# W_O read in joined pieces, the last V in one load, and a selection in two parts: an attention decode kernel on Trainium2

## The chip, the cores and the metric

One core of one Trainium2 chip. Its engines run their own instruction streams beside each other and meet at semaphores: TensorE (PE; PEld is its weight load) multiplies, VectorE (DVE), ScalarE (ACT) and GpSimd (POOL) work on elements, SyncE (SP) issues loads to 16 DMA engines. The metric is the device time of one execution in microseconds (us), lower is better. Times of before: 195.54 us, median of 3 runs (195.34 to 196.03).

## The reference

One decode step for 4 sequences: grouped-query attention over the last 4096 cached positions, plus a SwiGLU feed-forward, both on the same normalized input, plus the input itself.

```python
def _A_ref(x, k_cache, v_cache, wq, wo):      
    W = min(4096, max(256, Sk // 4))
    q = (x @ wq).reshape(B, Sq, Hq, Dh).transpose(0, 2, 1, 3)
    k = jnp.repeat(k_cache[:, :, Sk - W:, :], rep, axis=1)
    v = jnp.repeat(v_cache[:, :, Sk - W:, :], rep, axis=1)
    p = _softmax(jnp.einsum("bhqd,bhkd->bhqk", q, k) * (Dh ** -0.5))
    o = jnp.einsum("bhqk,bhkd->bhqd", p, v)
    return o.transpose(0, 2, 1, 3).reshape(B, Sq, Hq * Dh) @ wo
def _B_ref(x, w_gate, w_up, w_down):
    return (_silu(x @ w_gate) * (x @ w_up)) @ w_down
...
return x + _A_ref(xn, ...) + _B_ref(xn, ...)
```

Here W = 4096, Hq = 32, eight key heads, Dh = 128, D = 512 and F = 1792. The keys and values that are used are 2 x 32 MB, the weights some 13 MB, all bf16.

## The kernel before, in words

**The loads.** All large loads go through SyncE's one queue, in the order written in its function: W_Q, the first two K, W_gate, W_up, then V and K in turn, W_down, the last V, W_O. A K or a V load ("piece" d of ND = 16) is 2 MB: two sequences of one key head. K is double-buffered by TensorE's count of transposes (s_tr), V by the count of finished P times V (s_pv). The helper load (L174) issues a load whose destination is written by partition (16 KB each for K and V) and whose source is named in longer runs (32 KB: FOLD = 2 partitions' worth), by replacing the source's access pattern. K, V and the three feed-forward weights go through it. Two loads don't: the last V, which load_v_half (L250) issues as four loads of 512 KB, two for each half of the positions, with semaphores d_v[1] and d_vz, so that the first half can be used while the second is on its way; and W_O, which load_wo (L257) issues as five loads.

**W_O's layout.** wo_ap (L167) puts rows 32p to 32p + 31 of W_O into partition p, one after another: W_O's 4096 rows are 128 partitions times NO = 32 rows. What is called row c in this document is that c-th row of all partitions, a 128 x 512 operand. WO_CUTS (L123) cuts the 32 rows into loads: 0 to 15, 16 to 25, 26 to 28, 29 and 30, 31.

**The loop.** For each d, TensorE transposes K (L407), VectorE copies it back (L321), TensorE makes scores, a row maximum is taken, ScalarE takes the exponential (L292), and TensorE forms the denominators and P times V. The loop runs 8 times over two d; behind it stand gate and up products, the last denominators and P times V (L482 to L484, which wait for d_v[1] and d_vz), and the 28 products of the down projection.

**The end.** OT holds the attention output with the head's 128 dimensions across the partitions, one column per head and sequence. But row c of W_O in partition p belongs to row 32p + c of W_O, that is to head p // 4, dimension 32 (p % 4) + c. So the output must be regrouped: four transposes (L492) turn OT into tr_ps with 32 heads across the partitions, VectorE copies it to OB (L372), and four selecting products (L498), with the tables of ones and zeros in rep, spread it into op_ps, 128 partitions by 32 rows by 4 sequences; VectorE copies that to OP (L374). out_rows (L189) then multiplies OP's row c by W_O's row c, two products each, waiting for a W_O load at each cut. Rows 0 to 15 come inside the Block, the others behind it; at the Block's end the engines meet. spin (L445) issues filler products whose result nobody reads: two behind the transposes, three behind the selecting products, three behind row 15. At last y is copied by VectorE and ScalarE (L511, L513) and stored.

The table rep is made by GpSimd at the start (L206, L220), ahead of s_const, for which TensorE's first transposes wait.

Of the kernel before, what the change touches and what calls it, by code (L numbers as in the profile page):

```python
# [7 lines left out]
ALU = mybir.AluOpType  # L8
# [4 lines left out]
def bass_parallel_sum__sliding_block_cached__swiglu_ffn__decode_kernel(  # L13
# [32 lines left out]
    WIDE = 64  # L46
    PS = SN + WIDE
    NO = HQ * Dh // 128
    SCALE = float(Dh) ** -0.5
    EPS = 1e-5  # L50
# [16 lines left out]
    ones = sb("ones", [128, 128], BF16)  # L67
    rep = sb("rep", [32, REP, 128], BF16)
    mkr = sb("mkr", [2, 128], BF16)
# [16 lines left out]
    OT = sb("oT", [128, B, REP + HQ], BF16)  # L86
    OB = sb("oB", [32, B, Dh], BF16)
    OP = sb("oP", [128, NO, B], BF16)
    ex = sb("ex", [128, NF, B], FP32)
    guT = sb("guT", [128, NF, B], BF16)  # L90
    qT = KT[:, 0:2048].bitcast(FP32)
    gT = WQ[:, 0:NF * 64].bitcast(FP32)
    uT = WQ[:, NF * 64:NF * 128].bitcast(FP32)
    I4 = sb("i4", [B, B], FP32)
    I4w = sb("i4w", [B, 64], BF16)
# [15 lines left out]
    up_ps = ps_kt[1][:, 0:NF * 32]  # L111
    tr_ps = kt_ps[2][0:32, 0:B, :]
    op_ps = ps_kt[3][:, 0:B * 32]

    def sem(name):
        return nc.alloc_semaphore(name=name)
# [5 lines left out]
    d_out = sem("d_out")  # L122
    WO_CUTS = (0, 16, 26, 29, 31, 32)  # L123
    d_wo = [sem("d_wo%d" % q) for q in range(len(WO_CUTS) - 1)]
    d_k = [sem("d_k%d" % s) for s in range(2)]
    d_v = [sem("d_v%d" % s) for s in range(2)]
    d_vz = sem("d_vz")
    s_const = sem("s_const")
# [24 lines left out]
    s_guT = sem("s_guT")  # L153
    s_t4 = sem("s_t4")
    s_ob = sem("s_ob")
    s_pm = sem("s_pm")
# [9 lines left out]
    wd_ap = B_w_down.rearrange("(p t) n -> p t n", t=NF)  # L166
    wo_ap = A_wo.rearrange("(p c) n -> p c n", c=NO)  # L167
# [21 lines left out]
    def out_rows(eng, c0, c1):  # L189
        for c in range(c0, c1):  # L190
            if c in WO_CUTS:
                eng.wait_ge(d_wo[WO_CUTS.index(c)], 16)
            for n in range(2):
                last = eng.matmul(ps_acc[64 * n:64 * n + B, 0:256], OP[:, c, :], WO[:, c, 256 * n:256 * n + 256],  # L194
                                  start=False, stop=True, skip_group_check=True)
        return last

    with nc.Block() as block:

        @block.gpsimd  # L200
        def _(eng):
# [3 lines left out]
            eng.memset(I4w[:], 0.0)  # L205
            eng.memset(rep[:], 0.0)  # L206
            eng.memset(ones[:], 1.0)
# [10 lines left out]
                              fill=1.0, base=0, channel_multiplier=1)  # L218

            eng.affine_select(rep[:], rep[:], pattern=[[1, REP], [-1, 128]], compare_op=ALU.not_equal,  # L220
                              fill=1.0, base=0, channel_multiplier=REP)

# [14 lines left out]
            eng.engine_nop().then_inc(d_v[1], 16)  # L237

        @block.sync
        def _(eng):  # L240
# [8 lines left out]

            def load_v_half(d, h, done):  # L250

                a = d % 2 * KVN + h * HKN
                for i in range(FOLD):
                    b = i * KVN + h * HKN
                    eng.dma_start(VB[i:128:FOLD, a:a + HKN], kv_ap(A_v_cache, d, FOLD)[:, :, b:b + HKN]).then_inc(done, 16)

            def load_wo(n):  # L257
                a, b = WO_CUTS[n], WO_CUTS[n + 1]
                eng.dma_start(WO[:, a:b, :], wo_ap[:, a:b, :]).then_inc(d_wo[n], 16)

# [11 lines left out]
            load(eng, WD[:], wd_ap, fold_rows(B_w_down)).then_inc(d_wd, 16)  # L272
            eng.wait_ge(s_pv, ND)
            load_v_half(ND - 1, 0, d_v[1])
            load_v_half(ND - 1, 1, d_vz)
            for n in range(len(d_wo)):
# [20 lines left out]
        def _(eng):  # L297
# [74 lines left out]
            eng.tensor_copy(OB[:], tr_ps).then_inc(s_ob, 1)  # L372
            eng.wait_ge(s_pm, 1)
            eng.tensor_copy(OP[:].rearrange("p c b -> p b c"), op_ps.rearrange("p (b c) -> p b c", b=B)).then_inc(s_op, 1)  # L374

        @block.tensor
        def _(eng):
# [102 lines left out]
            for n in range(2):  # L480
                mm(ps_acc[64 * n:64 * n + 64, 0:256], I4w[:], X[:, 256 * n:256 * n + 256], start=True)
            pv(1, 0, (8 * ND + 16 * FOLD, ND + 1))  # L482
            eng.wait_ge(d_vz, 16 * FOLD)
            pv(1, 1, None)  # L484
# [18 lines left out]
            eng.wait_ge(s_op, 1)  # L503
            out_rows(eng, 0, WO_CUTS[1])
            spin(3)

# [38 lines left out]
```

## Time and profile before

| what | value |
|---|---|
| median of 3 runs | 195.54 us (195.34 to 196.03) |
| the profiled execution | 195.45 us, of which its span is 194.2 us |
| TensorE busy, of the span | 164.6 us, 85% |
| VectorE busy | 115.3 us, 59% |
| ScalarE, GpSimd busy | 17.0 us, 10.5 us |
| moved by DMA | 81.10 MB, mean 418 GB/s over the span |
| loads of K, of V (first 15) | 2048 KB each, landed 12.5 and 11.2 us behind their issue |

The span goes from the first to the last instruction that the profiler recorded. In the page's rows an engine is busy when an instruction of it runs; matmuls are pipelined, so that a busy TensorE is not one at its peak, and which engine bounds the kernel has to be read from what waits for what.

### The profile page before, as it was taken

The page shows a single profiled execution, that of the slowest core. Times are in us where ns is not written, and L with a number is a line of the kernel's source. Part 1 is how long each engine was busy: PE and PEld are TensorE (multiplying, and loading weights), DVE is VectorE, ACT ScalarE, POOL GpSimd, SP SyncE. Part 2 cuts the span into 40 slices and gives each one's busy share as a digit, 9 for nine tenths or more (in the row PEclk, how much of TensorE's full clock was granted, in tenths as well). Part 3 has the DMA queues.
Part 4 walks back from the last instruction along what each step waited for, and adds up shares of the span by engine and source line. Part 5 has one row for each costly group of instructions (what it writes and reads, how often), then busy time and mean ns, then how long its engine had stood idle before and what let it go on. Part 6 is the DMA issues. An engine that isn't in the chain of part 4 may idle for free. (4 is left out here: it accounts for less than half of the span.)

```text
span 194.2 us, 7760 instructions
## 1 busy us (share of the span) xinstructions
PE 164.6 (85%) x3466; PEld 141.6 (73%) x3466; DVE 115.3 (59%) x250; ACT 17.0 (9%) x27; POOL 10.5 (5%) x23
## 2 busy tenths in 40 slices
PE   0127999739999989898989898989898989898995
PEld 0112988638989888888888887888788878887752
DVE  1004858517677767676767676767676767675610
ACT  6600010100110101010101010101010101010100
POOL 8930000000000000000000000000000000000000
PEclk9999999988999999999999999999999999999999
DMA  6999998999999999999999999999999999998992
GB/s 224 425 439 432 564 393 346 425 430 439 412 432 432 432 432 432 432 432 432 432 432 432 432 432 439 432 452 432 432 432 432 432 439 432 432 472 353 437 407 107
DMA packets 3830, 81.10 MB, mean 418 GB/s; under 512 B 712, under 2 KB 848, under 8 KB 1104
## 3 DMA queue, kind: packets, MB, share of 16 engines
q1 hardware_dynamic: 3808, 81.01, 97.4%
q8 instruction: 5, 0.08, 0.2%
q10 hardware_dynamic: 16, 0.01, 0.0%
q14 instruction: 1, 0.01, 0.0%
HBM read 81.01 MB, written 0.00 MB: 417 GB/s over the span
## 5 line engine op out<-in xcount | busy, mean ns | idle before, releaser
L321 DVE COPY kT<-ps_kt 128x1024 bf16<-128x1024 bf16 x128 | 79.9, 683 | 28.0 <-PE ps_kt L407 28.0
L407 PE MATMUL ps_kt<-ident,kbuf 128*128 128x128 bf16 x1024 | 65.6, 224 | 11.2 <-DMA kbuf<-in_A_k_cache_dram 10.3
L407 PEld LDWEIGHTS ps_kt<-ident,kbuf 128*128 128x128 bf16 x1024 | 60.0, 101 | 16.5 <-issue 16.5
L379 PE MATMUL ps_o<-p,vbuf 128*128 128x64 bf16 x1120 | 38.4, 193 | 0.0
L379 PEld LDWEIGHTS ps_s<-qz,kT 128*128 128x128 bf16 x1024 | 31.4, 98 | 6.8 <-issue 3.6
L379 PEld LDWEIGHTS ps_o<-p,vbuf 128*128 128x128 bf16 x1120 | 35.2, 98 | 1.1
L379 PE MATMUL ps_s<-qz,kT 128*128 x1024 | 34.8, 192 | 1.2
L292 ACT ACTIVATE p<-ps_s 128x512 bf16<-128x512 f32 x17 | 10.2, 597 | 161.9 <-PE ps_s L379 161.9
L326 DVE TENSOR_REDUCE rm<-ps_s 128x8 bf16<-128x512 f32 x17 | 11.8, 691 | 19.9 <-PE ps_s L379 19.9
L379 PE MATMUL ps_kt<-wq_sb,xnT 128*32 128x512 bf16 x32 | 3.6, 629 | 5.5 <-DMA wq_sb<-in_A_wq_dram 5.5
L379 PE MATMUL ps_o<-p,ones 128*128 128x128 bf16 (+1 forms) x69 | 7.0, 222 | 1.6 <-DVE qz L312 1.3
L379 PE MATMUL ps_s<-mkc,mkr 2*128 2x512 bf16 x17 | 6.8, 398 | 0.0
L384 PE MATMUL ps_acc<-i,xn 4*128 4x4 f32 x4 | 0.6, 254 | 7.1 <-ACT xn L289 7.1
L379 PE MATMUL ps_s<-dg,ones 8*128 8x512 bf16 x17 | 6.5, 385 | 0.0
L379 PEld LDWEIGHTS ps_o<-p,ones 128*128 128x128 bf16 x69 | 4.5, 98 | 2.7 <-issue 2.2
L379 PEld LDWEIGHTS ps_kt<-wq_sb,xnT 128*32 128x32 bf16 x32 | 1.2, 137 | 7.1 <-issue 7.1
L309 DVE STREAM_TRANSPOSE kT<-ps_kt 128x512 f32<-128x512 f32 x2 | 1.4, 718 | 8.3 <-PE ps_kt L379 8.3
L384 PEld LDWEIGHTS ps_acc<-i,xn 4*128 4x128 f32 x4 | 0.6, 207 | 7.0 <-issue 7.0
L337 DVE TENSOR_REDUCE den<-ps_o 128x8 f32<-128x128 f32 x18 | 5.0, 275 | 1.0 <-PE ps_o L379 1.0
L234 POOL MEMSET vbuf<- 128x6144 f32 x1 | 5.2, 5222 | 0.0
L331 DVE TENSOR_REDUCE m<-ps_acc 8x1 f32<-8x128 f32 x17 | 4.6, 270 | 0.3 <-PE ps_acc L379 0.3
L341 DVE TENSOR_TENSOR oT<-ps_o,den 128x8 f32 (+1 forms) x18 | 3.0, 167 | 2.9 <-issue 2.7
(68 smaller groups left out, 50.5 us busy)
## 6 DMA issues: line engine op xcount, KB each, us to landing
kbuf<-in_A_k_cache_dram SPq DMA_DIRECT2D x16, 2048.0 KB, 12.5
vbuf<-in_A_v_cache_dram SPq DMA_DIRECT2D x15, 2048.0 KB, 11.2
wq_sb<-in_A_wq_dram SPq DMA_DIRECT2D x1, 4096.0 KB, 12.3
vbuf<-in_A_v_cache_dram SPq DMA_DIRECT2D x4, 512.0 KB, 7.8
wo_sb<-in_A_wo_dram SPq DMA_DIRECT2D x1, 2048.0 KB, 13.3
wg_sb<-in_B_w_gate_dram SPq DMA_DIRECT2D x1, 1792.0 KB, 24.1
wu_sb<-in_B_w_up_dram SPq DMA_DIRECT2D x1, 1792.0 KB, 27.5
wd_sb<-in_B_w_down_dram SPq DMA_DIRECT2D x1, 1792.0 KB, 14.9
```

What stands on the lines that cost most here:

```text
L234: eng.memset(VB[:, HKN:].bitcast(FP32), 0.0)
L292: eng.activation(P[:, d % 2 * PS:d % 2 * PS + SN], ps_S[d % 2][:], ACT.Exp, scale=SCALE).then_inc(s_p, 1)
L309: eng.transpose(qT[:, 512 * n:512 * n + 512], ps_kt[n][:])
L321: eng.tensor_copy(KT[:, u * HKN + 1024 * g:u * HKN + 1024 * (g + 1)], kt_ps[g].rearrange("p a b -> p (a b)")).then_inc(s_ev, 1)
L326: eng.tensor_reduce(RM[:], ps_S[bank][:].rearrange("p (t c) -> p c t", c=C), AX.X, ALU.max).then_inc(s_rm, 1)
L331: eng.tensor_reduce(m8[:], mt_ps, AX.X, ALU.max)
L337: eng.tensor_reduce(den[:], den_ps.rearrange("p (t c) -> p c t", c=C), AX.X, ALU.add)
L341: eng.tensor_tensor(OT[:, 2 * b:2 * b + 2, ds(r * REP, REP)], O_ps.rearrange("p (j h) -> p j h", j=2), den[:].rearrange("p (j h) -> p j h" ...
L379: return eng.matmul(o, l, r, start=start, stop=stop, skip_group_check=True)
L384: last = eng.transpose(xT_ps[:, c * B:(c + 1) * B], xn[:].rearrange("b (p c) -> b c p", c=NC)[:, c, :], I4[:])
L407: last = eng.transpose(kt_ps[g][:, k, :], KB[:, a:a + 128], ident[:])
```

## The change

- **Layout of W_O.** Rows 0 to 15 of a partition are now 16 neighbouring rows out of W_O's first 2048; rows 16 to 23 are 8 neighbouring rows out of the next 1024; rows 24 to 31 are one row of each of the last eight heads, 128 rows of W_O per load. The cuts become 0, 16, 24, 29, 31, 32; the last eight rows are eight loads that add to three semaphores.
- **Reads.** All W_O loads go through load: the first two name the source in runs of 32 KB, the last eight in 16 runs of 8 KB, with 1 KB written to each partition.
- **The last V** goes through load_v like the others: one load, one semaphore; d_vz is gone.
- **The regrouping.** The last eight heads need none: their operand is OT itself. The other NP = 24 are transposed, copied and selected in two parts (RUNS): 8 products with 64 columns for rows 0 to 15, then 16 products with 32 columns for rows 16 to 23, each part with its own copy to OP.
- **Fillers.** The three behind the selecting products and the three behind row 15 are gone; the two behind the transposes stay.
- **The tables** are made by GpSimd behind the Q projection (it waits for s_q = 2), in a part of WQ that is free by then; TensorE waits for s_rep ahead of the selecting.

```diff
+    RUNS = ((0, 16), (16, 8))
+    NP = 24
...
-    OB = sb("oB", [32, B, Dh], BF16)
-    OP = sb("oP", [128, NO, B], BF16)
+    OB = sb("oB", [NP, B, Dh], BF16)
+    OP = sb("oP", [128, NP, B], BF16)
...
+    rep_all = WQ[0:NP, NF * 128:NF * 128 + NP * 128]
+    rep = [rep_all[:, 1024 * n:1024 * n + 128 * (128 // r)].rearrange("a (e m) -> a e m", m=128)
+           for n, (_, r) in enumerate(RUNS)]
...
-    tr_ps = kt_ps[2][0:32, 0:B, :]
-    op_ps = ps_kt[3][:, 0:B * 32]
+    tr_ps = kt_ps[2][0:NP, 0:B, :]
+    op_ps = [t[:, 0:B * r].rearrange("p (b c) -> p b c", b=B) for t, (_, r) in zip((ps_kt[3], ps_kt[1]), RUNS)]
...
-    WO_CUTS = (0, 16, 26, 29, 31, 32)
+    WO_CUTS = (0, 16, 24, 29, 31, 32)
...
     def out_rows(eng, c0, c1):
         for c in range(c0, c1):
             if c in WO_CUTS:
-                eng.wait_ge(d_wo[WO_CUTS.index(c)], 16)
+                n = WO_CUTS.index(c)
+                eng.wait_ge(d_wo[n], 16 if c < NP else 16 * (WO_CUTS[n + 1] - c))
             for n in range(2):
-                last = eng.matmul(ps_acc[64 * n:64 * n + B, 0:256], OP[:, c, :], WO[:, c, 256 * n:256 * n + 256],
-                                  start=False, stop=True, skip_group_check=True)
+                last = eng.matmul(ps_acc[64 * n:64 * n + B, 0:256], OP[:, c, :] if c < NP else OT[:, :, REP + c],
+                                  WO[:, c, 256 * n:256 * n + 256], start=False, stop=True, skip_group_check=True)
...
         def _(eng):
-            eng.memset(rep[:], 0.0)
-            eng.affine_select(rep[:], rep[:], pattern=[[1, REP], [-1, 128]], compare_op=ALU.not_equal,
-                              fill=1.0, base=0, channel_multiplier=REP)
...
+            eng.wait_ge(s_q, 2)
+            eng.memset(rep_all.bitcast(FP32), 0.0)
+            eng.drain()
+            for (h, r), to in zip(RUNS, rep):
+                eng.affine_select(to, to, pattern=[[1, 128 // r], [-1, 128]], compare_op=ALU.not_equal,
+                                  fill=1.0, base=-128 // r * h, channel_multiplier=128 // r)
+            eng.drain()
+            eng.engine_nop().then_inc(s_rep, 1)
...
             def load_wo(n):
                 a, b = WO_CUTS[n], WO_CUTS[n + 1]
-                eng.dma_start(WO[:, a:b, :], wo_ap[:, a:b, :]).then_inc(d_wo[n], 16)
+                if a < NP:
+                    w = A_wo[128 * a:128 * b, :]
+                    load(eng, WO[:, a:b, :], w.rearrange("(p c) n -> p c n", p=128),
+                         w.rearrange("(p c) n -> p (c n)", c=32)).then_inc(d_wo[n], 16)
+                    return
+                for c in range(a, b):
+                    w = A_wo[128 * c:128 * c + 128, :]
+                    load(eng, WO[:, c, :], w, w.rearrange("(p c) n -> p (c n)", p=16)).then_inc(d_wo[n], 16)
...
-            eng.wait_ge(s_pv, ND)
-            load_v_half(ND - 1, 0, d_v[1])
-            load_v_half(ND - 1, 1, d_vz)
+            load_v(ND - 1)
...
-            eng.wait_ge(s_pm, 1)
-            eng.tensor_copy(OP[:].rearrange("p c b -> p b c"), op_ps.rearrange("p (b c) -> p b c", b=B)).then_inc(s_op, 1)
+            for n, (h, r) in enumerate(RUNS):
+                eng.wait_ge(s_pm, n + 1)
+                eng.tensor_copy(OP[:, h:h + r, :].rearrange("p c b -> p b c"), op_ps[n]).then_inc(s_op, 1)
...
-            pv(1, 0, (8 * ND + 16 * FOLD, ND + 1))
-            eng.wait_ge(d_vz, 16 * FOLD)
+            pv(1, 0, (8 * ND + 16, ND + 1))
             pv(1, 1, None)
...
-                    OT[:, i, REP:], ident[:])
+                    OT[:, i, REP:REP + NP], ident[:])
             last.then_inc(s_t4, 1)
             spin(2)
+            eng.wait_ge(s_rep, 1)
             eng.wait_ge(s_ob, 1)
-            for e in range(REP):
-                last = mm(op_ps.rearrange("p (b c) -> p b c", b=B), rep[:, e, :], OB[:, :, 32 * e:32 * e + 32],
-                          start=(e == 0))
-            last.then_inc(s_pm, 1)
-            spin(3)
+            for n, (h, r) in enumerate(RUNS):
+                for e in range(128 // r):
+                    last = mm(op_ps[n], rep[n][:, e, :], OB[:, :, r * e:r * e + r], start=(e == 0))
+                last.then_inc(s_pm, 1)
             eng.wait_ge(s_op, 1)
             out_rows(eng, 0, WO_CUTS[1])
-            spin(3)
+            eng.wait_ge(s_op, 2)
```

More of the change, by code (lines that the diff above doesn't have):

```diff
@@ L67, in bass_parallel_sum__sliding_block_cached__swiglu_ffn__decode_kernel @@
     ones = sb("ones", [128, 128], BF16)
-    rep = sb("rep", [32, REP, 128], BF16)
     mkr = sb("mkr", [2, 128], BF16)
@@ L126, in bass_parallel_sum__sliding_block_cached__swiglu_ffn__decode_kernel @@
     d_v = [sem("d_v%d" % s) for s in range(2)]
-    d_vz = sem("d_vz")
     s_const = sem("s_const")
@@ L154, in bass_parallel_sum__sliding_block_cached__swiglu_ffn__decode_kernel @@
     s_t4 = sem("s_t4")
+    s_rep = sem("s_rep")
     s_ob = sem("s_ob")
@@ L166, in bass_parallel_sum__sliding_block_cached__swiglu_ffn__decode_kernel @@
     wd_ap = B_w_down.rearrange("(p t) n -> p t n", t=NF)
-    wo_ap = A_wo.rearrange("(p c) n -> p c n", c=NO)
     ds = bass.ds
@@ L248, in load_v @@
                 load_kv(eng, VB, A_v_cache, d).then_inc(d_v[d % 2], 16)
[L250 to L255, printed above, removed]
             def load_wo(n):
                 a, b = WO_CUTS[n], WO_CUTS[n + 1]
-                eng.dma_start(WO[:, a:b, :], wo_ap[:, a:b, :]).then_inc(d_wo[n], 16)
+                if a < NP:
[6 more added lines that the diff above has]
+                    load(eng, WO[:, c, :], w, w.rearrange("(p c) n -> p (c n)", p=16)).then_inc(d_wo[n], 16)
             eng.dma_start(WQ[:], wq_ap).then_inc(d_wq, 16)
```

## The prediction

> **What bounds the kernel now.** I began with the head of the page and its DMA rows, to see which resource is never free.
>
> ```profile
> span 194.2 us, 7760 instructions
> GB/s 224 425 439 432 564 393 346 425 430 439 412 432 432 432 432 432 432 432 432 432 432 432 432 432 439 432 452 432 432 432 432 432 439 432 432 472 353 437 407 107
> q1 hardware_dynamic: 3808, 81.01, 97.4%
> q8 instruction: 5, 0.08, 0.2%
> PE ps_acc L194 1%; DVE y_sb L511 0%
> ```
>
> The loads issued by SyncE keep all 16 DMA engines busy for 97.4% of the span, at a flat 432 GB/s until the last slice. The page's chain is 1% long: it stops where the last W_O products begin, because what released them is a load. So I read the tail by itself, in the timeline (start, duration, engine, line, what; in brackets the idle time before and its releaser):
>
> ```profile
> 187.33 1.65 PEld L194 LDWEIGHTS ps_acc<-wo_sb,oP 128*4 128x4 bf16 x32 [0.65 <-DVE oP L374]
> 187.36 1.91 PE L194 MATMUL ps_acc<-wo_sb,oP 128*4 128x256 bf16 x32 [0.19 <-DMA wo_sb<-in_A_wo_dram]
> 190.32 1.30 PEld L194 LDWEIGHTS ps_acc<-wo_sb,oP 128*4 128x4 bf16 x26 [0.79 <-DMA wo_sb<-in_A_wo_dram]
> 190.33 2.11 PE L194 MATMUL ps_acc<-wo_sb,oP 128*4 128x256 bf16 x32 [0.30 <-PEq L198]
> 191.84 0.09 PEld L194 LDWEIGHTS ps_acc<-wo_sb,oP 128*4 128x4 bf16 x4 [0.23 <-DMA wo_sb<-in_A_wo_dram]
> 192.16 0.08 PEld L194 LDWEIGHTS ps_acc<-wo_sb,oP 128*4 128x4 bf16 x2 [0.23 <-DMA wo_sb<-in_A_wo_dram]
> 192.48 0.41 DVE L511 CAST y_sb<-ps_acc 4x256 bf16<-4x256 f32 x1 [5.58 <-PE ps_acc L194]
> ```
>
> The last two weight loads wait for W_O. The issue times of the five W_O loads (timeline of SyncE) and their times to landing (DMA view, whose last column counts from the issue):
>
> ```profile
> 173.94 0.59 SPq L259 DMA_DIRECT2D wo_sb<-in_A_wo_dram  x1
> 175.05 0.43 SPq L259 DMA_DIRECT2D wo_sb<-in_A_wo_dram  x1
> 176.00 0.43 SPq L259 DMA_DIRECT2D wo_sb<-in_A_wo_dram  x1
> ...
> wo_sb<-in_A_wo_dram SPq DMA_DIRECT2D x1, 2048.0 KB, 13.3
> wo_sb<-in_A_wo_dram SPq DMA_DIRECT2D x1, 384.0 KB, 16.2
> wo_sb<-in_A_wo_dram SPq DMA_DIRECT2D x1, 128.0 KB, 16.1
> ```
>
> The first lands at 173.94 + 13.3 = 187.24, the third at 175.05 + 16.2 = 191.25, the last at 176.00 + 16.1 = 192.10, and the last weight load starts at 192.16. The whole kernel is one stream of 81 MB, then 0.06 us, two products, two copies and the store. Whatever the change does must show in how long the stream takes, or in TensorE becoming later than the stream.
>
> **The reads (the same bytes in other pieces).** The last V goes from four loads with 8 KB runs to one with 32 KB runs, like the other V loads; W_O rows 0 to 15 from 16 KB to 32 KB runs; rows 16 to 31 from runs of 10, 3, 2 and 1 KB to 32 KB (rows 16 to 23) and 8 KB (eight loads of 128 KB, which still write 1 KB to each partition). What run length is worth stands in the windows view (last column GB/s, the one before it the DMA share):
>
> ```profile
> 100.00:140.00 40.00, 36.54 (x811) 32.82 (x812) 27.10 (x58) 2.39 (x4) 0.00 (x0) 1.00 1.00 433
> 177.00:180.00 3.00, 2.22 (x57) 1.61 (x57) 1.69 (x6) 0.33 (x1) 0.00 (x0) 1.00 1.02 431
> 182.00:186.00 4.00, 4.00 (x92) 3.13 (x88) 2.04 (x8) 0.00 (x0) 0.00 (x0) 1.00 1.01 429
> 189.70:191.70 2.00, 1.70 (x28) 1.08 (x26) 0.00 (x0) 0.00 (x0) 0.00 (x0) 1.00 0.52 193
> ```
>
> 32 KB runs move 433 GB/s (100 to 140 us, K and V alone), 8 KB runs 431 (177 to 180, the last V), 16 KB runs 429 (182 to 186, W_O). The stream is at its ceiling whatever the run. For 2 MB (2.097 MB): 4.84 us at 433, 4.87 at 431, 4.89 at 429. So the last V saves 0.03 us and rows 0 to 15 save 0.05. Rows 16 to 31 took 192.10 - 187.24 = 4.86 us. Afterwards rows 16 to 23 take 1.049 MB / 433 = 2.42 us. For the eight small loads the trace has no case of 8 KB read and 1 KB written at once. If the read sets the price, 8 x 0.131 MB / 431 = 2.43 us, in all 4.85, a saving of 0.01. If the 1 KB writes set it, the nearest rows are the last two loads, with runs of 2 and 1 KB on both sides: 0.256 + 0.128 MB in 192.10 - 191.25 = 0.85 us, 0.283 us per 128 KB, eight times that 2.27. That lies under the streaming price, since in these last 2 us the engines run out one by one (share 0.52), so it bounds from below. From above I bound it by the slowest pace that a row shows for one load, its issue on SyncE: 0.43 us, eight times that 3.44. Nothing in the rows points to that end: the loads of 3, 2 and 1 KB came at the stream's own rate. I take the read price: together -0.09 us, bounds -0.25 and +0.92.
>
> [...]
>
> **SyncE.** Four V and five W_O issues become one and ten, 11 for 9, at 0.43 to 0.6 us each: the last starts at about 176.00 + 2 x 0.6 = 177.2, some 14 us ahead of its landing. At the Block's end TensorE meets SyncE, but at 189 or later. Cost nothing; uncovered, each issue would cost its 0.43 us, the upper bound above.
>
> **The path through TensorE.** The last V in one load means the first half can't be used earlier. The rows of before (SyncE's third and fourth V issue with their landings, then the timeline):
>
> ```profile
> L255 SPq DMA_DIRECT2D vbuf<-in_A_v_cache_dram x2: 599/599/599, 172.7 to 173.3; - x2
> ...
> DMA to landing us min/median/max: 7.9/8.4/8.8
> ```
> ```profile
> 181.42 0.40 PE L379 MATMUL ps_o<-p,ones 128*128 128x128 bf16 x4
> 181.60 1.96 PEld L379 LDWEIGHTS ps_o<-p,vbuf 128*128 128x128 bf16 x64
> ...
> 186.03 0.22 PEld L379 LDWEIGHTS ps_kt<-oB,rep 32*128 32x128 bf16 x4 [0.46 <-DVE oB L372]
> 186.35 0.33 PEld L379 LDWEIGHTS ps_s<-kbuf,ident 128*128 128x128 bf16 x3
> 186.46 0.44 DVE L374 CAST oP<-ps_kt 128x128 bf16<-128x128 f32 x1 [0.49 <-PE ps_kt L379]
> ```
>
> The V is complete at 173.3 + 8.8 = 182.1 and stays there; the denominators that began at 181.42 now begin at about 182.1, +0.65, and all behind them on TensorE (P times V, the 28 down products, the transposes) moves with them, so the selecting starts at 186.03 + 0.65 = 186.68. Four selecting products of 128 columns took 186.35 - 186.03 = 0.32, 80 ns each; the new 8 and 16 have 64 and 32 columns, and the nearest row of that width is P times V, 1.96 / 64 = 31 ns. I take 31 (80 as the bound): 8 take 0.25 (0.64), all 24 take 0.74 (1.92). VectorE's copy of the first half (64 of 128 columns, 0.22 to 0.44) runs beside the 16. The first 16 W_O rows start at 186.68 + 0.74 + 0.1 = 187.5 (bound 188.7), against 187.33, where they too had waited for W_O's landing at 187.24. They need 1.65; the three filler products behind them are gone, the Block's end costs 0.30 as now: 189.5 (190.7). Rows 16 to 23, 16 products at 1.65 / 32 = 52 ns, are done at 190.3 (191.5). The loads of rows 24 to 28 are due at about 192.1 - 3 x 0.3 = 191.2. So TensorE still waits for the stream, with 0.9 us to spare; at the bound the last 16 products, 0.83 us, end at 192.3 where they now end at 192.24. Cost nothing, bound +0.1.
>
> **GpSimd.** The table of ones moves from the start (0.51 + 0.62 us) to behind the Q projection, three and six times as long:
>
> ```profile
> 1.10 0.51 POOL L206 MEMSET rep<- 32x512 bf16 x1
> 2.97 0.62 POOL L220 TENSOR_SCALAR_AFFINE_SELECT rep<-rep 32x512 bf16<-32x512 bf16 x1
> 4.91 0.60 SPq L178 DMA_DIRECT2D wu_sb<-in_B_w_up_dram  x1
> 23.43 0.55 SPq L178 DMA_DIRECT2D vbuf<-in_A_v_cache_dram  x1
> wu_sb<-in_B_w_up_dram SPq DMA_DIRECT2D x1, 1792.0 KB, 27.5
> ```
>
> About 1.5 + 3.7 = 5.3 us near 17 to 22 us, needed 165 us later. If it held VectorE up for all of it, the first V would go out at 28.7 instead of 23.43; the load ahead of it in the stream lands at 4.91 + 27.5 = 32.4. Nothing.
>
> **Sum.** -0.09 us against this execution, 195.45 us for its span of 194.2 (1.25 around it), so 195.36; the median shown, 195.54, lies 0.09 above it and gives 195.45. I predict 195.5.
>
> **The rivals.** The page has five refills of instructions (queue 8), and two fall in the tail, one in 182 to 184 and one in 190 to 191.5:
>
> ```profile
> q8 instruction: 1, 0.02, 3.1%
> ...
> q8 instruction: 1, 0.02, 3.9%
> ```
>
> 3.1% of 16 engines over 2 us is 1.0 us of one engine; each load is split over the 16 once, so an engine that lost 1.0 us stays behind. The share of 0.52 in the last 2 us says that the engines do end up to 2 us apart; together they would end after 1.04 of these 2 us.
> - Faster: the engine that ends last loses its handicap (the refill comes elsewhere because TensorE is 0.65 later there, or the bigger pieces even it out). Up to 0.96 us off: 194.5. For it: the idle half. Against: the code up to that point is the same. Chance 0.12.
> - Slower: TensorE has 14 more products ahead of the second refill (20 more to select, 6 fewer fillers), which moves it from 190.1, with the engines running empty, to near 189, inside the stream. It decides if it hits an engine that is less than 1.0 us ahead of the last one; at most +0.94: 196.4. Against: half of the engines' time in the last 2 us is idle, so many end well ahead. Chance 0.07.
> - Slower: the eight small loads run at SyncE's issue pace, 8 x 0.43 = 3.44 us, or by their writes, for 2.43: +1.0, 196.5. Against: 431 GB/s at 8 KB. Chance 0.06. [...]
> - Slower: without fillers the clock falls. After 2.94 us without work it was at 0.72 over 6 us, and 32 transposes took 3.42 us:
>
> ```profile
> 42.45 3.42 PE L407 MATMUL ps_kt<-ident,kbuf 128*128 128x128 bf16 x32 [2.94 <-DMA kbuf<-in_A_k_cache_dram]
> 42.00:48.00 6.00, 5.55 (x90) 5.10 (x91) 3.81 (x9) 0.00 (x0) 0.00 (x0) 0.72 1.01 437
> ```
>
> The longest gaps of the tail would be 0.65 and 0.9 us. If it fell at 187.5 and products took half as long again, TensorE would end about 1 us late: 196.5. Chance 0.02.
> - That the change does nothing measurable, since joining reads gains only where run length costs, is the forecast itself: 0.73.
>
> **How the numbers follow.** What a measurement of this kernel can't tell from no change is 0.3%, 0.59 us. The forecast's own range, 195.2 to 195.9, is -0.25 and, for half of the small loads' bound, +0.46 about the value. To leave out no more than 2 in 10, the range reaches to 194.7 and 196.4. Faster by over 0.3%: most of the first rival, 0.13 with a tail of the forecast. Slower: 0.14. Within: 0.73.
>
> **What would show it.** Right: the last weight load of W_O still waits for DMA and starts within 0.3 us of 192.16; GB/s stays near 431 to the end; the denominators start near 182.1 and the first W_O products near 187.5. Wrong: windows under 400 GB/s before 189 (small loads), an idle time before the last rows that names OP's copy (selecting too slow), PEclk under 1.00 behind 187, or a last landing moved by over 0.6 us with the same rates, which is the engines' spread.

## The result, and the profile after

The changed kernel took 196.84 us (median of 22 runs, 196.24 to 199.83) against 195.56 us (median of 22, 195.32 to 197.91) for the kernel before. The ratio is 1.0055, 95% interval 1.0038 to 1.0073: slower by about half a per cent, more than the 0.3% that can be told from no change, and outside the predicted range of 194.7 to 196.4. A few of the 22 runs of each were disturbed (two of the changed kernel took 199.8 us); the ratio leaves them out.

The profiled execution is 1.3 us longer than that of before (spans 195.5 and 194.2). These are lines of its page: the head, the busy times, the DMA rate in 40 slices, and the queue of SyncE's loads.

```profile
span 195.5 us, 7797 instructions
...
PE 163.3 (84%) x3479; PEld 141.3 (72%) x3480; DVE 115.4 (59%) x251; ACT 17.0 (9%) x27; POOL 13.9 (7%) x24
...
GB/s 229 429 443 436 545 379 384 443 427 436 409 443 429 436 429 429 429 429 429 429 429 436 429 429 436 436 429 429 429 429 429 436 429 429 429 456 436 426 297 76
...
q1 hardware_dynamic: 3232, 81.01, 97.3%
```

The same 81.01 MB went in 3232 packets where it took 3808, and the engines were busy for the same share, 97.3%. Up to the 38th slice the mean rate is that of before (427 GB/s against 426). The last two slices moved 297 and 76 GB/s, against 407 and 107: the loss is in the last 10 us. There the timeline of TensorE's weight loads reads (start, duration, line, what; in brackets the idle time before and its releaser):

```profile
182.10 0.23 PEld L389 LDWEIGHTS ps_o<-p,ones 128*128 128x128 bf16 x4 [0.83 <-DMA vbuf<-in_A_v_cache_dram]
...
186.78 0.71 PEld L389 LDWEIGHTS ps_kt<-oB,wq_sb 24*128 24x128 bf16 x24 [0.53 <-issue]
187.59 1.62 PEld L200 LDWEIGHTS ps_acc<-wo_sb,oP 128*4 128x4 bf16 x32
191.07 0.74 PEld L200 LDWEIGHTS ps_acc<-wo_sb,oP 128*4 128x4 bf16 x16 [1.86 <-DMA wo_sb<-in_A_wo_dram]
192.59 0.64 PEld L200 LDWEIGHTS ps_acc<-wo_sb,oT 128*4 128x4 bf16 x14 [0.78 <-DMA wo_sb<-in_A_wo_dram]
193.43 0.09 PEld L200 LDWEIGHTS ps_acc<-wo_sb,oT 128*4 128x4 bf16 x2 [0.20 <-DMA wo_sb<-in_A_wo_dram]
```

TensorE is ready for rows 16 to 23 at 189.2 and waits 1.86 us for them; the last weight load starts at 193.43, 1.27 us behind the 192.16 of before, and all of its waits name W_O. The issues of the first, second and last W_O load (timeline of SyncE), with the times to landing of the three sizes (DMA view; the third row is the median of the eight small loads):

```profile
171.99 0.60 SPq L183 DMA_DIRECT2D wo_sb<-in_A_wo_dram  x1
172.63 0.60 SPq L183 DMA_DIRECT2D wo_sb<-in_A_wo_dram  x1
177.70 0.59 SPq L183 DMA_DIRECT2D wo_sb<-in_A_wo_dram  x1
...
wo_sb<-in_A_wo_dram SPq DMA_DIRECT2D x1, 2048.0 KB, 15.0
wo_sb<-in_A_wo_dram SPq DMA_DIRECT2D x1, 1024.0 KB, 18.4
wo_sb<-in_A_wo_dram SPq DMA_DIRECT2D x8, 128.0 KB, 16.1
```

Rows 0 to 15 land at 171.99 + 15.0 = 186.99, 0.25 us earlier than before. Rows 16 to 23 land at 172.63 + 18.4 = 191.03. The last small load, issued at 177.70, is there when the last weight load starts, at 193.43. From 186.99 to 193.4 the same 2 MB took 6.4 us that had taken 4.86.

One stretch shows it best: 187.5 to 190.5 us, when all engines still have work (windows view; the last two columns are the DMA share and GB/s). A packet, one read by one engine, counts whole in the stretch in which it starts, so that a share can pass 1.00 and that share and rate are best read together. The kernel before:

```profile
187.50:190.50 3.00, 2.70 (x39) 1.60 (x37) 0.00 (x0) 0.00 (x0) 0.00 (x0) 1.00 0.94 377
```

The changed kernel:

```profile
187.50:190.50 3.00, 2.00 (x36) 1.32 (x32) 0.26 (x2) 0.00 (x0) 0.00 (x0) 1.00 0.99 262
```

The engines are busier than before and move less: per byte a transfer holds its engine (0.99 / 262) / (0.94 / 377) = 1.5 times as long. A stream that runs out of work shows a lower share, as before's does from 189.7 to 191.7 us: 0.52, at 193 GB/s. The packets themselves, which the traces keep one by one, say the same: the 128 reads of 8 KB held their engines for 0.44 us on average (0.31 to 0.64), while every 8 KB read of before, in its last V, took 0.31. So the question was what makes these transfers long.

### The profile page after: what moved, and what is told of

Its sections match the earlier page's. It is cut to its first block, busy times and chain, and to the rows that moved or that the text cites. A ratio compares the mean times of both kernels' runs of the same rounds, so it can differ in the third digit from the quotient of the medians.

```text
span 195.5 us, 7797 instructions
## 1 busy us (share of the span) xinstructions
PE 163.3 (84%) x3479; PEld 141.3 (72%) x3480; DVE 115.4 (59%) x251; ACT 17.0 (9%) x27; POOL 13.9 (7%) x24
## 3 DMA queue, kind: packets, MB, share of 16 engines
q1 hardware_dynamic: 3232, 81.01, 97.3%
HBM read 81.01 MB, written 0.00 MB: 414 GB/s over the span
## 4 chain that ended last, share of the span: by engine, by line
DMA 61%; PE 33%; SPq 2%; DVE 2%; issue 2%; DVEq 0%
DMA kbuf<-in_A_k_cache_dram 46%; PE ps_kt L417 17%; DMA wo_sb<-in_A_wo_dram 9%; PE ps_s L389 8%; DMA wq_sb<-in_A_wq_dram 6%; PE ps_o L389 6%; SPq L183 2%; PE ps_kt L389 2%; PE ps_acc L389 1%; DVE kT L330 1%; PE ps_acc L200 1%; DVE kT L318 0%; DVE qz L321 0%; DVE y_sb L520 0%; DVEq L329 0%
## 5 line engine op out<-in xcount | busy, mean ns | idle before, releaser
L417 PE MATMUL ps_kt<-ident,kbuf 128*128 128x128 bf16 x1024 | 64.0, 221 | 11.1 <-DMA kbuf<-in_A_k_cache_dram 10.2
L417 PEld LDWEIGHTS ps_kt<-ident,kbuf 128*128 128x128 bf16 x1024 | 58.3, 99 | 16.2 <-issue 16.2
L389 PE MATMUL ps_o<-p,vbuf 128*128 128x64 bf16 x1120 | 39.9, 196 | 0.0
L389 PEld LDWEIGHTS ps_o<-p,vbuf 128*128 128x128 bf16 x1120 | 36.7, 100 | 1.2
## 6 DMA issues: line engine op xcount, KB each, us to landing
wo_sb<-in_A_wo_dram SPq DMA_DIRECT2D x1, 1024.0 KB, 18.4
```

Of the source, the lines that this page charges most:

```text
L389: return eng.matmul(o, l, r, start=start, stop=stop, skip_group_check=True)
L417: last = eng.transpose(kt_ps[g][:, k, :], KB[:, a:a + 128], ident[:])
```

## The experiments

Unless a sentence says otherwise, each kernel is the changed one with the edit shown. Most numbers stand in a table at the end of this section; the kernel before took 195.27 to 195.6 us beside them, and ratios are to its runs on the same chip.

**1. What about the small loads?** Three theories: A, that each small load reads one stretch of 128 KB; B, that one 8 KB read is joined from eight rows and written in eight pieces of 1 KB; C, that eight loads of 128 KB in a row are simply many small loads. The first kernel reads every row for itself:

```diff
-                    load(eng, WO[:, c, :], w, w.rearrange("(p c) n -> p (c n)", p=16)).then_inc(d_wo[n], 16)
+                    eng.dma_start(WO[:, c, :], w).then_inc(d_wo[n], 16)
```

> The changed kernel, but each of the last eight W_O loads reads 128 runs of 1 KB instead of 16 runs of 8 KB; the same 128 KB stretch of memory, the same 1 KB writes. Theory A (all 16 engines read inside one 128 KB stretch at the same time, and that stretch can't be read faster): still slow, 230 to 300 GB/s behind 187.5 us, last W_O products near 193.4, about 196.8 us. Theory B (a long read that is split into eight short writes is slow): each load takes 0.35 us as the 1 KB load of before did, last products near 192.3, about 195.6 us. Theory C (many small loads are slow by themselves): slow, as A.

The second keeps the 16 reads of 8 KB, but takes them 256 KB apart; its last eight rows of W_O hold other rows of W_O.

```diff
-                    load(eng, WO[:, c, :], w, w.rearrange("(p c) n -> p (c n)", p=16)).then_inc(d_wo[n], 16)
+                    f = 8 * (c - NP)
+                    load(eng, WO[:, c, :], A_wo[f:f + 128, :],
+                         A_wo.rearrange("(p r) n -> p (r n)", p=16)[:, f * D:(f + 8) * D]).then_inc(d_wo[n], 16)
```

> The changed kernel, but the 16 runs of 8 KB of each of the last eight loads lie 256 KB apart in W_O instead of next to each other, so that these eight rows of W_O are the wrong ones; sizes, writes and counts of loads as in the changed kernel. Theory A: fast, 0.31 to 0.33 us per load, over 400 GB/s up to 189.5, last products near 192.1, about 195.5 us. Theory B and theory C: slow, last products near 193.4, about 196.8 us.

The third is the kernel before with eight loads of one row at the end, and nothing else changed:

```diff
-    WO_CUTS = (0, 16, 26, 29, 31, 32)
+    WO_CUTS = (0, 16, 24, 25, 26, 27, 28, 29, 30, 31, 32)
```

> The kernel before, with W_O's rows 16 to 31 cut into one load of 8 rows and eight loads of one row (128 KB each, 128 runs of 1 KB that lie 32 KB apart). Theory C: the eight loads are slow, last products near 193.4, about 196.8 us. Theories A and B: 0.35 us per load, 8 x 0.35 = 2.8 us for what took 2.6, last products near 192.4, about 195.7 us.

The fourth is the kernel before with the last V in one load:

```diff
-            eng.wait_ge(s_pv, ND)
-            load_v_half(ND - 1, 0, d_v[1])
-            load_v_half(ND - 1, 1, d_vz)
+            load_v(ND - 1)
...
-            pv(1, 0, (8 * ND + 16 * FOLD, ND + 1))
-            eng.wait_ge(d_vz, 16 * FOLD)
+            pv(1, 0, (8 * ND + 16, ND + 1))
```

> The kernel before, with the last V in one load. If the later start of the last P times V (near 182.1 instead of 181.42) costs nothing, as predicted, the last W_O products start within 0.15 us of 192.16, about 195.5 us; the rival, that TensorE's path becomes the later one, has the first W_O products near 188.0 and the end up to 0.65 us later, 196.1 us.

Plain reads give all of the loss back: ratio to the kernel before 0.9999 (0.9983 to 1.0015). Reads 256 KB apart are as slow as neighbouring ones, 1.0073 (1.0047 to 1.0099), so A falls. Eight small loads in the old layout cost nothing, 1.0008 (0.9988 to 1.0027), so C falls. What is left is B, the joined read.

The last V in one load shows no cost in time, 1.0005 (0.9982 to 1.0028), but its profile has the sign of the rival that its expectation names:

```profile
187.97 1.62 PEld L194 LDWEIGHTS ps_acc<-wo_sb,oP 128*4 128x4 bf16 x32 [0.42 <-DVE oP L372]
...
190.90 1.65 PEld L194 LDWEIGHTS ps_acc<-wo_sb,oP 128*4 128x4 bf16 x32 [0.76 <-DMA wo_sb<-in_A_wo_dram]
```

The first W_O products come at 187.97, and the last 32 run in one piece to 192.55, where before's end at 192.24 behind two more waits. In the layout of before the one load makes TensorE end 0.3 us later in this profile, no longer held by the last loads.

**2. How long may the joined read be?** Besides, D: that loads through the helper are slow whatever they join. One number in the edit of the first kernel changes, the p of the source, in how many runs the 128 KB are read: 128 (1 KB each, only the helper stays), 64 (2 KB, two writes) and 32 (4 KB, four writes).

```diff
-                    load(eng, WO[:, c, :], w, w.rearrange("(p c) n -> p (c n)", p=16)).then_inc(d_wo[n], 16)
+                    load(eng, WO[:, c, :], w, w.rearrange("(p c) n -> p (c n)", p=128)).then_inc(d_wo[n], 16)
```

> The changed kernel, but the source of the last eight W_O loads is named in 128 runs of 1 KB while they still go through the helper load, so that reads and writes have the same length but the instruction is of the helper's kind. Theory B (a read that is split into several short writes is slow): fast as the plain rows were, last products near 192.4, about 195.6 us. Theory D (loads through the helper reach the DMA engines more slowly, whatever their lengths): slow, under 300 GB/s behind 187.5, last products near 193.4, about 196.8 us.

> The changed kernel with 64 runs of 2 KB per small load, two writes of 1 KB to a read. Theory B with a cost that grows with the number of writes to a read: between e1 (0.35 us per load) and the changed kernel (about 0.5), so 195.7 to 196.2 us. Theory B with a cost that depends on the lengths differing at all, and theory D: as slow as the changed kernel, about 196.8 us.

> The changed kernel with 32 runs of 4 KB per small load, four writes of 1 KB to a read. Theory B with a cost that grows with the number of writes: slower than with two, 196.0 to 196.6 us. Otherwise about 196.8 us.

The fourth joins longer pieces: rows 24 to 30 in one load of 16 reads of 56 KB, each written in eight pieces of 7 KB, with row 31 plain; rows 24 to 30 hold other rows of W_O.

```diff
-    WO_CUTS = (0, 16, 24, 29, 31, 32)
+    WO_CUTS = (0, 16, 24, 31, 32)
...
+                w = A_wo[128 * a:128 * b, :]
+                if b < NO:
+                    load(eng, WO[:, a:b, :], w.rearrange("(p c) n -> p c n", p=128),
+                         w.rearrange("(p c) n -> p (c n)", p=16)).then_inc(d_wo[n], 16)
+                else:
+                    eng.dma_start(WO[:, a, :], w).then_inc(d_wo[n], 16)
```

> The changed kernel with rows 24 to 30 in one load that takes 16 runs of 56 KB and writes 7 KB to each partition (seven neighbouring rows of W_O per partition, so these rows are the wrong ones for their heads), and row 31 by plain 1 KB runs. The ratio of eight writes to a read stays, the writes are long and the small loads are gone. If the ratio alone is slow: 0.9 MB at about 250 GB/s is 3.7 us, last products near 193.3, about 196.7 us. If it is the short writes (theory B) or the number of small loads through the helper (theory D): full rate, 2.1 us, the last load near 191.7, last products near 192.3; TensorE then has 14 products to do behind the seven rows' landing, which end by 192.6: 195.5 to 195.9 us.

The helper costs nothing (0.9993, 0.9966 to 1.002): D falls. Two and four writes to a read cost nothing that can be told (1.0021, 0.9994 to 1.0047, and 0.9997, 0.9963 to 1.003). The window of the kernel with four writes:

```profile
187.50:190.50 3.00, 2.70 (x59) 2.00 (x56) 0.53 (x2) 0.00 (x0) 0.00 (x0) 1.00 0.92 361
```

361 GB/s with four, 262 with eight: no slope, a step. In the packets of these kernels an engine was held, per KB, for 46 ns by the plain reads of 1 KB, 42 by reads of 2 KB, 41 by reads of 4 KB, and 55 by the 8 KB reads of the changed kernel; before's plain 8 KB reads took 39 and the 32 KB reads 38. And the pieces need not be short nor the loads small. With pieces of 7 KB in one load of 896 KB the ratio is 1.0175 (1.0108 to 1.0243), in these weight loads:

```profile
191.91 0.74 PEld L200 LDWEIGHTS ps_acc<-wo_sb,oP 128*4 128x4 bf16 x16 [2.56 <-DMA wo_sb<-in_A_wo_dram]
194.49 1.37 PEld L200 LDWEIGHTS ps_acc<-wo_sb,oT 128*4 128x4 bf16 x16 [1.83 <-DMA wo_sb<-in_A_wo_dram]
```

Rows 16 to 23, whose own load is unchanged, take 19.1 us from issue to landing, 0.7 more than in the changed kernel: what follows them in the queue holds them up. Not all of the loss is the stream's. Behind these waits the granted clock (third column from the end) falls, and 16 products take 1.87 us that took 1.04:

```profile
191.91 1.04 PE L200 MATMUL ps_acc<-wo_sb,oP 128*4 128x256 bf16 x16 [2.27 <-DMA wo_sb<-in_A_wo_dram]
194.49 1.87 PE L200 MATMUL ps_acc<-wo_sb,oT 128*4 128x256 bf16 x16 [1.54 <-DMA wo_sb<-in_A_wo_dram]
...
195.00:197.00 2.00, 1.36 (x14) 0.52 (x10) 0.41 (x1) 0.38 (x1) 0.00 (x0) 0.50 0.00 0
```

That is 0.8 us of some 3.4. The expectation for slow reads was 196.7, so this kernel is slower than any theory had it. So B in its first form, short writes, falls too. What the two slow forms share is that a read covers eight neighbouring partitions.

**3. Is it where the writes go?** Theory P, the author's conjecture: which partitions are written decides, and the same bytes cost more in 0 to 63 than in 32 to 95, by long reads as by plain ones. The rival, R, is that the form of the reads alone decides. All four kernels are the one with plain rows (1. above) plus one load of 448 KB of W_O into a free part of K's buffer, behind rows 16 to 23, whose data nobody uses; its bytes alone are worth 0.459 MB / 433 = 1.06 us. It goes to partitions 0 to 63 or 32 to 95 (o = 0 or 32), as 8 reads of 56 KB that cover eight partitions each, or as 64 plain runs of 7 KB.

```diff
...
+                if n == 2:
+                    eng.wait_ge(s_tr, 2 * NG * ND)
+                    m = A_wo[0:448, :]
+                    to, rows = KB[o:o + 64, KVN:KVN + 7 * D], m.rearrange("(p c) n -> p (c n)", p=64)
+                    load(eng, to, rows, m.rearrange("(p c) n -> p (c n)", p=8)).then_inc(d_more, 16)
...
+    nc.sync.wait_ge(d_more, 16)
```

In the plain two the line with load is

```diff
+                    eng.dma_start(to, rows).then_inc(d_more, 16)
```

> The kernel of e1 (last eight rows of W_O by plain 1 KB runs) plus one more load between W_O's rows 16 to 23 and these: 448 KB into partitions 0 to 63 of a K buffer that is free by then, named as 8 reads of 56 KB with eight writes of 7 KB each. [...]

> The same with partitions 32 to 95 in place of 0 to 63; sizes, reads and writes are the same. [...] Theory R: as slow as e9.

> The same extra load into partitions 0 to 63, but by 64 plain runs of 7 KB, one write to a read. [...] Theory R: full rate, 1.06 us, about 196.6 us.

> As e11 with partitions 32 to 95. [...] Theory R: the same, as e11.

The plain pair is the cleanest: the same bytes, the same reads, the same place in the queue, 32 partitions further on. One execution each: 200.1 us into 0 to 63, 196.84 into 32 to 95; so the views of the tail count for more here than the two times. Window and landing of the extra load into 0 to 63:

```profile
187.50:190.50 3.00, 1.99 (x35) 1.33 (x32) 0.25 (x2) 0.00 (x0) 0.00 (x0) 1.00 0.94 171
...
kbuf<-in_A_wo_dram SPq DMA_DIRECT2D x1, 448.0 KB, 18.8
```

and into 32 to 95:

```profile
187.50:190.50 3.00, 2.70 (x54) 1.95 (x51) 0.46 (x2) 0.00 (x0) 0.00 (x0) 1.00 0.93 356
...
kbuf<-in_A_wo_dram SPq DMA_DIRECT2D x1, 448.0 KB, 15.4
```

The engines are equally busy and move half as much: which partitions are written decides. The load lands 3.4 us later behind its issue, and its 7 KB reads held their engines for 0.52 us (median) into 0 to 63 and 0.27, every one of them, into 32 to 95. R has no answer to that: it had the full rate in both, and the runs moved 171 and 356 GB/s. Why 0 to 63 are slower they don't show.

The plain 1 KB reads behind the extra load were held up too, 66 ns against 46 (medians), and after a wait of 2.7 us the last 16 products ran at a granted clock of 0.50, as in the kernel with 56 KB reads.

The pair with long reads did not come out as P wanted: 199.97 us into 0 to 63, but also 200.72 into 32 to 95. Either long reads are slow wherever they go, or the loads behind them slowed these. Both of these kernels too ended at a clock of 0.50.

**4. Neighbouring partitions, or something else about the reads?** Theory N: a read is slow when its writes go to eight neighbouring partitions. First test: keep the 8 KB and the eight writes of 1 KB, but to four neighbouring partitions, in two rows each. R expects that to be slow. The last eight rows of W_O are loaded in pairs c, c + 4, and hold other rows of W_O.

```diff
-    WO_CUTS = (0, 16, 24, 29, 31, 32)
+    WO_CUTS = (0, 16, 24, 25, 26, 27, 28)
...
+                w = A_wo[128 * NP + 256 * (a - NP):128 * NP + 256 * (b - NP), :]
+                load(eng, WO[:, a:a + 5:4, :], w.rearrange("(p c) n -> p c n", p=128),
+                     w.rearrange("(p o c) n -> p o (c n)", p=32, o=1)).then_inc(d_wo[n], 16)
```

> The changed kernel with its last eight rows of W_O in four loads of 256 KB instead of eight of 128 KB: each load fills two rows that are four apart (24 and 28, and so on), in 32 reads of 8 KB, and each read has eight writes of 1 KB, to four neighbouring partitions, two rows in each (so these rows are other rows of W_O than the reference's). Theory N (a read is slow when its writes go to eight neighbouring partitions): fast, 0.61 to 0.66 us per load, last products near 192.4, about 195.6 us. Theory R (eight writes to a read are slow): as slow as the changed kernel, under 300 GB/s behind 187.5, about 196.8 us.

The other two put the extra load of long reads at the very end of the stream, with nothing behind it:

> The kernel of e10 with the extra load (8 reads of 56 KB into partitions 32 to 95) behind the eight rows, last in the stream. [...]

> The kernel of e9 with the extra load (partitions 0 to 63) last in the stream. [...] Theory R: as e14.

Eight writes to four partitions are fast:

```profile
187.50:190.50 3.00, 2.66 (x53) 1.90 (x51) 0.50 (x2) 0.00 (x0) 0.00 (x0) 1.00 0.87 344
```

0.87 / 344 is 1.01 times the engine time per byte of before, where the changed kernel had 1.5. The time is 1.0027 (1.0016 to 1.0037); some of what remains has another place, the tail of TensorE:

```profile
192.54 0.42 PEld L200 LDWEIGHTS ps_acc<-wo_sb,oT 128*4 128x4 bf16 x10 [0.54 <-DMA wo_sb<-in_A_wo_dram]
```

Ten products stand behind the last landing, 0.42 us, where there are two, 0.09, in the changed kernel. The reads of 8 KB held their engines for 0.33 us on average, against 0.44 in the changed kernel.

The two with the extra load at the end took 196.27 us (32 to 95) and 196.7 (0 to 63), one execution each. Over 186 to 196 us the engines' share is 0.58 with the first,

```profile
186.00:196.00 10.00, 5.63 (x95) 3.40 (x92) 1.36 (x4) 0.38 (x1) 0.00 (x0) 0.95 0.58 215
```

and 0.63 with the second:

```profile
186.00:196.00 10.00, 6.11 (x103) 3.81 (x98) 1.35 (x4) 0.38 (x1) 0.00 (x0) 0.94 0.63 218
```

The difference is 0.05 x 16 x 10 = 8 us of engine time, but less than half of it is the extra load's: the second run's stream is 0.45 us late ahead of the load (its last V is issued at 171.90, not 171.45), so that more of what comes ahead falls into the window. The two times differ by no more than this lateness and say nothing on P. The packets do: the eight reads took 2.32 to 2.84 us into 32 to 95 (mean 2.47) and 2.32 to 3.48 into 0 to 63 (mean 2.95), about 0.5 us each for the partitions alone, and the last one 2.32 in both. P holds for long reads too, with nothing behind them. By R the reads take as long in both, so R falls here as well. Between the two kernels with long reads to 32 to 95 only the place in the queue differs, and there the reads took 3.63 us on average with the eight rows behind them, and 2.47 with nothing behind: the place in the queue costs them 1.16 us each, and 2.47 is 0.35 above the 2.12 us of the 56 KB reads over four partitions.

**5. Or the number of reads?** One gap was left: every joined load that cost time had 16 reads or fewer, and every one that cost none had 32 or more. Theory O: a load with one read for each engine is what costs. The first kernel keeps 16 reads of 8 KB in a load, each to four partitions in two rows, for partitions 32 to 95 of the pairs; partitions 0 to 31 and 96 to 127 are two plain loads. The second is its control, all three plain.

```diff
-                load(eng, WO[:, a:a + 5:4, :], w.rearrange("(p c) n -> p c n", p=128),
-                     w.rearrange("(p o c) n -> p o (c n)", p=32, o=1)).then_inc(d_wo[n], 16)
+                for lo, hi in ((0, 32), (32, 96), (96, 128)):
+                    v = w[2 * lo:2 * hi, :]
+                    to, rows = WO[lo:hi, a:a + 5:4, :], v.rearrange("(p c) n -> p c n", p=hi - lo)
+                    if lo == 32:
+                        load(eng, to, rows, v.rearrange("(p o c) n -> p o (c n)", p=16, o=1)).then_inc(d_wo[n], 16)
+                    else:
+                        eng.dma_start(to, rows).then_inc(d_wo[n], 16)
...
```

> As the run with 32 reads of 8 KB to four partitions (W_O's last eight rows in four pairs c and c + 4), but the middle 64 partitions (32 to 95) of each pair are one load of 16 reads of 8 KB, each written to four neighbouring partitions in eight pieces of 1 KB; partitions 0 to 31 and 96 to 127 of the pair are two plain loads. The last eight rows of W_O hold other rows of W_O, as in that run. Theory N (what costs is a read that covers eight neighbouring partitions): four partitions, so no stretch: over 335 GB/s in 187.5 to 190.5 us, the time within 0.4 us of the kernel with the same loads all plain, about 196.0. Rival O (what costs is a load with only 16 reads, one for each engine): the middle half of the bytes is stretched as in the changed kernel, so about half of its loss, 0.6 to 0.7 us: under 310 GB/s, about 0.6 us longer than the plain one.

> The same three loads for each pair of W_O's last rows, all plain (runs of 2 KB read, two pieces of 1 KB written); the last eight rows hold other rows of W_O. Both theories: 343 GB/s or more in 187.5 to 190.5 us and about 196.0 us, as with 32 reads; it is what the other run is held against, since partitions 0 to 31 and 96 to 127 as loads of their own may cost something in both.

Sixteen reads to four partitions:

```profile
187.50:190.50 3.00, 2.19 (x44) 1.50 (x40) 0.46 (x2) 0.00 (x0) 0.00 (x0) 1.00 1.00 284
```

The same loads plain:

```profile
187.50:190.50 3.00, 2.18 (x44) 1.49 (x40) 0.44 (x2) 0.00 (x0) 0.00 (x0) 1.00 1.03 281
```

The two are equal, 197.41 and 197.4 us, 1.0085 (1.0056 to 1.0114) and 1.0089 (1.0058 to 1.0121), where O wanted 0.6 us between them; they give it nothing. The control itself missed its expectation of 196.0 us. With loads to 32, 64 and 32 partitions plain runs move 281 GB/s, and their 1 KB reads were held for 57 ns on average instead of 46; that fits P, if what a load as a whole covers matters as well, but nothing else was changed to test it. It also means that O was tested inside an already slowed stream, so it is not excluded with the same weight as A, C and D.

| kernel | time, us | ratio to before | share and GB/s, 187.5 to 190.5 us |
|---|---|---|---|
| before | 195.56 | | 0.94, 377 |
| changed | 196.84 | 1.0055 | 0.99, 262 |
| changed, rows plain (128 reads) | 195.6 | 0.9999 | 0.97, 344 |
| changed, 128 reads by the helper | 195.56 | 0.9993 | 0.98, 348 |
| changed, 64 reads | 196.05 | 1.0021 | 0.93, 353 |
| changed, 32 reads | 195.66 | 0.9997 | 0.92, 361 |
| changed, 16 reads of 56 KB | 199.4 | 1.0175 | 0.77, 178 |
| changed, 32 reads to 4 partitions x 2 rows | 196.02 | 1.0027 | 0.87, 344 |
| plain rows + 448 KB to 0-63, 8 reads | 199.97 | one execution | 0.96, 225 |
| plain rows + 448 KB to 32-95, 8 reads | 200.72 | one execution | 1.02, 241 |
| plain rows + 448 KB to 0-63, plain | 200.1 | one execution | 0.94, 171 |
| plain rows + 448 KB to 32-95, plain | 196.84 | one execution | 0.93, 356 |

The times of the kernel with 16 reads of 56 KB and of the first three of the last four contain the 0.8 us of the fallen clock. No version is faster than before. The best, with reads of 1 KB or 4 KB, equal it.

## Why the prediction was wrong

**The step that failed** is the price of the eight small loads in "The reads". It was taken as the read's, 2.43 us, with an upper bound of 3.44 us from SyncE's issue pace. Rows 16 to 23 and the small loads were to take 4.85 us together and took 6.4. The reads of the small loads by themselves held each engine for 128 x 0.44 / 16 = 3.5 us. Nor did the bound for the loss, +0.92 us, hold: the last weight load came 1.27 us late. The step looked for the price in the length of the reads, the length of the writes and the pace of the issues, and the runs show that none of these costs anything that the time tells: four-write reads 0.9997, plain reads and writes of 1 KB 0.9999, loads of 128 KB in the old layout 1.0008. Its remark that the loads of 3, 2 and 1 KB came at the stream's own rate is a little off, since their reads held an engine for 40, 42 and 46 ns per KB against 38 for the 32 KB reads; but that isn't what failed.

The step didn't ask which partitions a read covers once runs are joined. In before's W_O loads every read goes to one partition, in the joined K and V loads to two, in the feed-forward weights (56 KB) to four. After the change it is two in rows 0 to 15, four in rows 16 to 23, and eight in the last eight loads. The number stood in the diff: 128 partitions in 16 runs.

The same step also charged the loss to the wrong place. Rows 16 to 23, priced at 2.42 us (to 189.7), landed at 191.03, though their own form is sound. The small loads behind them in the queue slow them down: the first 8 KB read starts at 187.47 us, while reads of rows 16 to 23 still run, and the last of these take up to 2.15 us, where a 32 KB read takes 1.21. Removing only the joining of the last eight brings the whole 1.24 us back (196.84 to 195.6).

**The rival that was nearest**, small loads at 196.5 with a chance of 0.06, had the right place and about the right time, but neither of its mechanisms. The issues were through at 178.3, 15 us ahead of the last landing, and plain 1 KB writes cost nothing that the time tells. The sign "windows under 400 GB/s before 189 (small loads)" was the useful one: it fired at once.

**What was right.** Rows 0 to 15 landed no later: 186.99, 0.25 us earlier than before, where 0.08 was predicted for them and V together; but with the same loads up to there they landed at 187.27 in the kernel with plain rows, so the 0.25 is no gain that can be told. The denominators began at 182.10 (182.1), the selecting at 186.78 (186.68), the 24 products took 0.71 us (0.74, from the nearest row of that width), and the first W_O products came at 187.59 (187.5). TensorE waited for the stream from then on, with 1.86, 0.78 and 0.20 us. SyncE's last issue started at 177.70 (177.2). GpSimd's tables took 1.37 + 3.06 us from 16.69 us on (5.3 estimated), and the first V went out at 23.49 (23.43). That the later start of P times V is hidden holds in the changed layout: with 128 reads by the helper all four weight loads behind row 15 wait for W_O (0.57, 0.53, 0.21 and 0.24 us). The kernel of before with V in one load doesn't bear it out by itself, as shown above.

**The other rivals.** The clock stayed at 1.00 through the window, with no fillers and a gap of 1.86 us. What the rival on the clock describes did come in experiments with longer waits: 0.50 behind gaps of 2.56 and 1.83 us. The second refill of instructions was to come near 189, inside the stream. It came at about 191, when TensorE had waited for rows 16 to 23 (DMA view, 190.9 to 191.5 us):

```profile
q1 hardware_dynamic: 42, 0.14, 68.0%
q8 instruction: 1, 0.02, 11.8%
```

Whether the engine that ended last lost its handicap can't be seen: the loss is larger.

**What is shown and what is argued.** Shown: that the loss is in the joining of the last eight loads; that a step lies between four and eight neighbouring partitions to a read (361 and 344 GB/s against 262); that at equal reads and bytes the partitions written decide the rate (171 against 356 GB/s). The kernel before already had a pair for the step: its feed-forward weights come in 56 KB reads over four partitions, 2.12 us each, where the 56 KB reads over eight took 3.87 (medians). The cause is not shown, neither of this step nor of the difference between 0 to 63 and 32 to 95: no view here shows which engine wrote which partition. Open stays why the long reads to 32 to 95 took 3.63 us each with other loads behind them and 2.47 at the end of the stream. Whether 16 reads to a load would cost anything in an undisturbed stream wasn't tried.

## What to carry to other kernels

When the source of a load is named in longer runs than the destination's partitions, count the partitions that one run covers and let it be four at most: with four the window moved 361 and 344 GB/s here, with eight 262 and 178. A gain from longer runs is only there if the rate shows a loss to begin with: here 1 KB reads hold an engine for 46 ns per KB and 32 KB reads for 38, and on the last 1 MB the kernel's time didn't show the difference. And write to all 128 partitions in one load where the stream is the bound: partitions 0 to 63 alone halved the rate (171 GB/s against 356 into 32 to 95), and loads to 32, 64 and 32 partitions came with 281 where loads to all 128 had 344, while the engines looked fully busy (0.94 and 1.03).

## What was not expected of the hardware

- A busy share near 1.0 says nothing about the rate. The share was 0.94 both at 171 GB/s (448 KB into partitions 0 to 63) and at 377 GB/s (before); only GB/s beside it tells the slowed stream from the full one.
- A slow load slows the loads ahead of it. Rows 16 to 23, loaded alike in all of these, took 16.7 us from issue to landing with plain rows behind them, 18.4 with reads over eight partitions and 19.1 with seven rows of these in one load.
- Reads of 1 KB cost little in this stream: they hold an engine for 46 ns per KB against 38 for reads of 32 KB, and with 1024 of them in the last 1 MB the kernel took 195.6 us, against 195.56 us for the kernel before.
- A long wait can cost twice: behind gaps of 2.56 and 1.83 us the granted clock was 0.50, and 16 products took 1.87 us in place of 1.04.
- Eight loads of 128 KB at the end of a full queue cost nothing: 1.0008 and 0.9993.
